# Splitting the first K block's load into four row-quarters and putting one of them ahead of wq in a GQA decode kernel

## The chip, the cores and the metric

The kernel runs on one core of one Trainium2 chip. The metric is the device time of one execution in microseconds. The core has five engines that run side by side and wait for one another through semaphores: PE (matrix products; PEld is its weight load), DVE (vector operations), ACT (activation functions; it also issues DMAs here), POOL and SP (which here only issues DMAs). All DMAs of the core run on the same 16 DMA engines. Data is kept on the chip in 128 partitions.

## The reference

One token `x` of 448 numbers is decoded. An attention part `a` runs over a long cache, a small token mixer `b` runs beside it, and a gate mixes the two.

```python
g = _sigmoid((x * gate_w).sum(-1, keepdims=True))
q = (x @ wq).reshape(B, Sq, Hq, Dh)                # 16 heads of 256
k, v = repeat(k_cache, 2), repeat(v_cache, 2)      # 8 K/V heads, 65536 keys each
scores = einsum("bhqd,bhkd->bhqk", q, k) * (Dh ** -0.5)
a = einsum("bhqk,bhkd->bhqd", _softmax(scores), v).reshape(B, Sq, Hq * Dh) @ wo
h = _layernorm(x)
u = _gelu(einsum("bsd,sf->bdf", h, w1) + b1)       # 1792 wide
b = (einsum("bdf,fs->bds", u, w2) + b2).transpose(0, 2, 1)
out = g * a + (1 - g) * b
```

Nearly all of the bytes are the two caches in bf16: 8 heads x 65536 keys x 256 numbers x 2 bytes, for K and again for V, 537 MB together.

## The kernel before, in words

The keys of each of the 8 K/V heads are cut into 4 blocks of 16384, which makes 32 blocks. A block of K is one transfer of 8 MB: 128 partitions, and in each a row of 64 KB that is contiguous in memory (128 keys of 256 numbers). A block of V is the same.

On the chip there are one buffer `vt` for a block of V and one tile `k_all` with three slots of half a block each (32 KB per partition). A block of K takes two neighbouring slots: even blocks slots 0 and 1, odd blocks slots 1 and 2. DVE transposes a K block in eight pieces (L410, tile `kT`), PE multiplies each piece with the query held in `qz` (L418), and when the eight are done the block's softmax follows (L475 to L514) and the products with V (L438). A loop over t (L605) runs two blocks per pass and 15 passes; the last two blocks are written out behind it.

SP issues all large transfers, in the order in which the program has them: within a block the next V is issued once PE has finished with `vt`, and the next K once DVE has transposed out of the slots that it will overwrite. Transfers that have been issued queue up on the DMA engines, so data flows without a gap as long as the next one is issued before the last has run dry.

Ahead of the loop stands a prelude, and it is what the change touches.

- `xr` (the token) is loaded by ACT's queue, and behind it small tables for the mixer and the gate.
- SP loads `wq` into the space of `vt` that V will use later: a piece `wq_t` of 0.5 MB and a piece `wq_m` of 3 MB (L167, L170). Then it loads K block 0 into slots 0 and 1 of `k_all` (`load_k_whole(0, 0)`, L182, recorded at L132).
- Slot 2 of `k_all` is not needed before block 1. The prelude uses it as scratch under the name `early`: `xf` is the token spread over the partitions (written at L266), `h_bc` its layer norm (L283), `gel` the 14 results of the gelu (ACT, L288), `zt` the gate's product (L346).
- DVE runs the layer norm from L266 to L283 in order; ACT's gelu follows; PE multiplies the queries out of wq (L299, L306), spreads them (L317) and sums the mixer (L352). `gate_sum` ends on ACT with `ez` (L348), and `mixer_tail` on DVE (L357 to L368) finishes the mixer's part.
- A barrier over the engines stands at the loop's entry. In the loop's first half pass PE spreads and applies `wo` (L563, L540, L554), SP issues V block 0 (`load_v`, recorded at L135), and DVE begins to transpose K block 0.

A helper `seq` keeps the instructions of each engine in the order in which they are written, on each side of the loop separately. Which instruction waits for which, and which semaphore it uses, the framework works out from the tiles that each one writes and reads. DMAs take eight semaphores in turn; a DMA that reuses a semaphore first waits for the DMA that had it before.

Of the kernel before, what the change touches and what calls it, by code (L numbers as in the profile page):

```python
# [21 lines left out]
KP = VP // 2  # L22
# [11 lines left out]
def kernel(  # L34
# [15 lines left out]
    nc = tc.nc  # L50
# [12 lines left out]
    def seq(ins):  # L63
        e = ins.ins.engine
        if e in last:
            tc.add_manual_dep(
                ins.ins,
                last[e],
                mybir.DependencyInfo(
                    mybir.DependencyClass.NoSync, mybir.DependencyReason.DATA  # L70
                ),
                reason="program order",
            )
        last[e] = ins.ins.name
        return ins
# [9 lines left out]
    k_all = kvpool.tile([128, 3 * KP, DH], BF16, name="k_all")  # L85
# [24 lines left out]
    DM = 384  # L110
    wq_m = vt[:, 0:48, :].rearrange("p a b -> p (a b)").rearrange("p (k n) -> p k n", k=3)
# [11 lines left out]
    def rows(name, n):  # L123
        return flat[name][bass.ds(n, 1)].rearrange("o p j d -> (o p) j d")
# [6 lines left out]
    def load_k_whole(n, slot):  # L131
        seq(nc.sync.dma_start(out=k_all[:, slot * KP:(slot + 2) * KP, :], in_=rows("k", n)))  # L132

    def load_v(n, j0=0, j1=VP):
        seq(nc.sync.dma_start(out=vt[:, j0:j1, :], in_=rows("v", n)[:, j0:j1, :]))  # L135

# [22 lines left out]
    def load_v_last(n):  # L159
# [4 lines left out]
            ))  # L164

    seq(nc.scalar.dma_start(out=xr[:], in_=A_x[0, 0].rearrange("(o n) -> o n", o=1)))
    seq(nc.sync.dma_start(  # L167
        out=wq_t[:, :], in_=A_wq[DM:D, :].rearrange("r (h n) -> (r h) n", h=2)
    ))
    seq(nc.sync.dma_start(out=wq_m, in_=A_wq[0:DM, :].rearrange("(p k) n -> p k n", k=3)))  # L170
    for k, table in enumerate((
        B_w1[0].rearrange("(b p) -> b p", p=128),
        B_b1.rearrange("(b p) -> b p", p=128),
# [3 lines left out]
    for n0, n1 in ((0, D // 2), (D // 2, D)):  # L177
        seq(nc.scalar.dma_start(
            out=gw[:, n0:n1], in_=gate_w.rearrange("(o n) -> o n", o=1)[:, n0:n1]
        ))  # L180
    seq(nc.scalar.dma_start(out=b2b[:], in_=B_b2.rearrange("(o n) -> o n", o=1)))
    load_k_whole(0, 0)  # L182


    steps = const.tile([128, WS + 128], BF16)
# [8 lines left out]
        out=val[:], in_=rowsel[:, :, :, 0:NI], op=ALU.add, axis=AXIS.XY  # L194
    ))
    fst = const.tile([128, 2, REP], FP32)
    for e in range(2):
        seq(nc.vector.tensor_reduce(
            out=fst[:, e, :], in_=rowsel[:, :, :, e:e + 1], op=ALU.add, axis=AXIS.XY
# [3 lines left out]
        out=par[:], in_=ident_f[:].rearrange("p (a r) -> p r a", r=REP), op=ALU.add, axis=AXIS.X  # L203
# [3 lines left out]
        out=nval[:], in0=val[:], scalar1=-scale, scalar2=None, op0=ALU.mult  # L207
# [7 lines left out]
        out=same[:], in_=val[:].unsqueeze(1).to_broadcast([128, 64, REP])  # L215
# [8 lines left out]
        out=sel[:],  # L224
        in_=ident.rearrange("p (w k) -> p w k", w=NW).unsqueeze(2).to_broadcast([128, NW, NQ, 32]),
# [7 lines left out]
        out=xrr[:], in_=xr[:, DM:D].unsqueeze(2).to_broadcast([1, D - DM, 2])  # L233
    ))
    x_col = hd_ps[:, 40:44]
    for k in range(3):
# [13 lines left out]
        out=xtm[:], in0=par[:], scalar1=x_col[:, 3:4], scalar2=None, op0=ALU.mult  # L250
# [19 lines left out]
        out=veps[:], in0=mv[:, 1:2], scalar1=1e-5, scalar2=None, op0=ALU.add  # L270
# [5 lines left out]
    for _ in range(2):  # L276
# [3 lines left out]
            out=ntmp[:], in0=ntmp[:], scalar1=-0.5, scalar2=1.5, op0=ALU.mult, op1=ALU.add  # L280
# [3 lines left out]
        out=h_bc, in0=xf, scalar1=mv[:, 0:1], scalar2=rstd[:, 0:1],  # L284
        op0=ALU.subtract, op1=ALU.mult,
    ))
    for b in range(NF):
        seq(nc.scalar.activation(  # L288
            out=gel[b], in_=h_bc, func=ACT.Gelu_apprx_tanh,
# [33 lines left out]
    for k in range(2):  # L323
        seq(nc.vector.tensor_copy(
            out=qq[:, :, :, k, :], in_=qq_ps.rearrange("p (w g r) -> p w g r", g=HKV, r=REP)
# [279 lines left out]
    with tc.For_i(0, HQ - 1, 1, iteration_sync="staggered") as t:  # L605
        for e in range(2):
            if e:
                tc.stage_boundary()
            if e == 0:
                spread_wo(1)  # L610
                head_end()
                older_wo()
            tc.previous_stage_wait(mybir.EngineType.Activation)
            score_block(
                e, (e, e + 1), early_signals(0), FORWARD if e else UPPER_FIRST
            )
            load_v(2 * t + e)
            tc.stage_boundary()
            if e == 0:
                load_k_whole(2 * t + 1, 1)  # L620
                load_wo_wide(t)
                softmax(e, may_begin=True)
                tc.previous_stage_wait(mybir.EngineType.DVE)
                tc.previous_stage_wait(mybir.EngineType.Activation)
                products(e)
            else:
                load_k_whole(2 * t + 2, 0)
                softmax(e, pair=t + 1)
                tc.previous_stage_wait(mybir.EngineType.DVE)
                tc.previous_stage_wait(mybir.EngineType.Activation)  # L630
                denominators()
                turn()
                products(e)
# [6 lines left out]
    for n in (L - 1, L):  # L640
# [4 lines left out]
        if n == L - 1:  # L645
            load_v(n, 0, 48)
            load_k(L, 0, 2)
            load_k(L, 1, 1)
            load_v(n, 48, VP)
        else:  # L650
            load_v_last(L)
            load_wo(HQ - 1, 1)
        if n < L:
            softmax(n % 2)
        else:
            def rest_base():
# [9 lines left out]
                out=lsv[:], in0=val[:], scalar1=lsum[:, 0:1], scalar2=None, op0=ALU.mult  # L666
# [8 lines left out]
                out=rdv[:], in0=rdv[:], scalar1=gcol[:, 0:1], scalar2=None, op0=ALU.mult  # L675
# [6 lines left out]
    for c in range(2):  # L682
# [9 lines left out]
        out=oT[:], in0=o_last, in1=rdv[:].unsqueeze(1).to_broadcast([128, 2, REP]), op=ALU.mult  # L692
# [43 lines left out]
```

## Time and profile before

| what | value |
|---|---|
| median of 3 runs | 1263.91 us (1263.62 to 1263.98) |
| span of the profiled execution, first to last instruction | 1261.8 us |
| time around the span (median less span) | 2.1 us |
| DMA | 544.36 MB, mean 431 GB/s over the span |
| PE busy | 824.5 us, 65% of the span |
| DVE busy | 711.8 us, 56% |
| ACT busy | 75.7 us, 6% |
| mean granted PE clock | 0.811 of full |

The profiled execution is one run of the same program; the page gives its span, and its own whole time is not listed beside it, so the span with the 2.1 us around it stands for it. A timeline row reads: start in us, length in us, engine, line, operation, tile written, tile read, how many were merged, and in brackets the idle time in front with what ended it. A row of DMA issues ends with the us from issue to landing.

### The profile page before, as it was taken

How to read it: one execution, taken by the hardware profiler on the slowest of the kernel's cores; microseconds unless marked ns; L12 is line 12 of the kernel's file. 1: busy time of each engine (PE TensorE's matmuls, PEld its weight loads, DVE VectorE, ACT ScalarE, POOL GpSimd, SP SyncE). 2: the span in 40 equal slices, each digit the busy share in tenths (PEclk: the TensorE clock that was granted, in tenths of full speed). 3: DMA queues.
4: the chain of work that ended last, by engine and by line, in shares of the span. 5: the costliest groups of instructions: out<-in, count | busy, mean ns of one | idle time of the engine just before them, and what ended most of it. 6: DMA issues, size and time to landing. Idle time of an engine off the chain costs nothing.

```text
span 1261.8 us, 12358 instructions
## 1 busy us (share of the span) xinstructions
PE 824.5 (65%) x4818; PEld 331.2 (26%) x4818; DVE 711.8 (56%) x755; ACT 75.7 (6%) x163; POOL 4.8 (0%) x9
## 2 busy tenths in 40 slices
PE   4757467575666756577566766658656576665668
PEld 2222122222222312223222322223222232222224
DVE  5665456654556644566544665445655456654575
ACT  4000000000000000000000000000000000000000
POOL 1000000000000000000000000000000000000000
PEclk8887788877787877978778887788877797877878
DMA  9999999999999999999999999999999999999998
GB/s 415 435 435 432 439 432 432 437 434 437 432 434 435 434 425 440 416 441 443 423 434 437 432 432 439 432 439 432 432 439 432 439 432 432 439 432 435 421 435 355
DMA packets 11624, 544.36 MB, mean 431 GB/s; under 512 B 1532, under 2 KB 1918, under 8 KB 2782
## 3 DMA queue, kind: packets, MB, share of 16 engines
q1 hardware_dynamic: 11522, 544.22, 99.6%
q8 instruction: 6, 0.10, 0.0%
q14 instruction: 4, 0.03, 0.0%
q10 hardware_dynamic: 92, 0.01, 0.0%
HBM read 544.22 MB, written 0.00 MB: 431 GB/s over the span
## 4 chain that ended last, share of the span: by engine, by line
DMA 67%; PE 14%; DVE 13%; issue 4%; ACT 0%; SPq 0%; DVEq 0%; ACTq 0%
DMA k_all<-in_A_k_cache_dram 67%; PE sc L418 13%; DVE kT L410 13%; PE hd_ps L463 0%; PE pv_last L438 0%; PE pv_last L563 0%; PE f L563 0%; DVE rmax L475 0%; PE hd_ps L684 0%; ACT p_sb L506 0%; PE hd_ps L554 0%; PE pv_ps L438 0%; PE f L697 0%; PE sm_ps L493 0%; DVE pT L513 0%
## 5 line engine op out<-in xcount | busy, mean ns | idle before, releaser
L418 PE MATMUL sc<-kT,qz 128*128 128x512 bf16 x2048 | 550.4, 419 | 315.0 <-DVE kT L410 314.8
L410 DVE STREAM_TRANSPOSE kT<-k_all 128x2048 f32<-128x2048 f32 x256 | 571.3, 2283 | 207.6 <-DMA k_all<-in_A_k_cache_dram 154.7
L418 PEld LDWEIGHTS <-qz 128*128 128x128 bf16 x2048 | 212.5, 104 | 651.3 <-issue 474.8
L438 PE MATMUL pv_ps<-vt,pT 128*4 128x512 bf16 x1968 | 172.0, 525 | 27.3 <-DVE pT L513 27.3
L519 DVE SCALAR_TENSOR_TENSOR acc<-acc,al,pv_ps 128x512 f32<-128x512 f32 x31 | 23.2, 747 | 160.4 <-PE pv_ps L438 160.4
L438 PEld LDWEIGHTS <-pT 128*4 128x4 bf16 x2000 | 56.5, 108 | 130.1 <-issue 83.9
L506 ACT ACTIVATE p_sb<-sc,nb 128x512 bf16<-128x512 f32 x32 | 22.0, 687 | 1020.0 <-DVE nb L502 1020.0
L475 DVE TENSOR_REDUCE rmax<-sc 128x1 f32<-128x512 f32 x32 | 22.1, 692 | 63.7 <-PE sc L418 63.7
L513 DVE STREAM_TRANSPOSE pT<-p_sb 128x512 bf16<-128x512 bf16 x32 | 22.8, 712 | 27.1 <-ACT p_sb L506 27.1
L525 PE MATMUL hd_ps<-lsum,same 128*128 128x1 f32 x30 | 8.2, 342 | 28.8 <-DVE lsum L514 28.8
L493 PE MATMUL sm_ps<-mrun,ones_f 1*128 1x2 f32 x64 | 12.1, 256 | 21.2 <-DVE mrun L492 13.0
L479 PE MATMUL sm_ps<-ident_f,rmax 128*1 128x128 f32 x32 | 8.6, 270 | 24.5 <-DVE rmax L475 24.5
L563 PE MATMUL pv_last<-wo_in,steps 128*128 128x448 bf16 x64 | 15.6, 368 | 5.5 <-PEq L605 5.5
L563 PEld LDWEIGHTS <-steps 128*128 128x128 bf16 x128 | 11.6, 101 | 22.6 <-issue 14.4
L493 PEld LDWEIGHTS sm_ps<-mrun,ones_f 1*128 1x128 f32 x64 | 9.4, 182 | 27.4 <-DVE mrun L492 16.3
L567 ACT CAST wo_sb<-pv_last 128x448 bf16<-128x448 f32 x16 | 8.5, 532 | 126.3 <-PE pv_last L563 126.3
L558 DVE TENSOR_TENSOR a_acc<-a_acc,hd_ps 1x448 f32<-1x448 f32 x15 | 9.1, 608 | 12.3 <-PE hd_ps L554 12.3
L554 PE MATMUL hd_ps<-wo_sb,oT 128*1 128x448 bf16 x60 | 15.8, 351 | 0.0
L563 PE MATMUL f<-wo_in,steps 128*128 128x448 bf16 x64 | 15.5, 367 | 0.0
L570 ACT COPY wo_sb<-wo_sb 128x896 bf16<-128x896 bf16 x15 | 14.1, 937 | 14.5 <-PE hd_ps L554 14.5
L525 PEld LDWEIGHTS hd_ps<-lsum,same 128*128 128x128 f32 x30 | 6.9, 285 | 30.1 <-DVE lsum L514 30.1
L550 DVE CAST oT<-hd_ps 128x2 bf16<-128x2 f32 x15 | 2.4, 160 | 20.8 <-PE hd_ps L540 20.8
(124 smaller groups left out, 194.6 us busy)
## 6 DMA issues: line engine op xcount, KB each, us to landing
k_all<-in_A_k_cache_dram SPq DMA_DIRECT2D x2, 4096.0 KB, 15.2
vt<-in_A_v_cache_dram SPq DMA_DIRECT2D x1, 5120.0 KB
k_all<-in_A_v_cache_dram SPq DMA_DIRECT2D x1, 4096.0 KB
wo_in<-in_A_wo_dram SPq DMA_DIRECT2D x15, 224.0 KB, 27.8
vt<-in_A_wq_dram SPq DMA_DIRECT2D x1, 3072.0 KB, 10.4
vt<-in_A_v_cache_dram SPq DMA_DIRECT2D x1, 3072.0 KB
k_all<-in_A_v_cache_dram SPq DMA_DIRECT2D x1, 2048.0 KB
k_all<-in_A_v_cache_dram SPq DMA_DIRECT2D x1, 1024.0 KB, 21.7
```

The costliest lines, as they stand in the source:

```text
L410: seq(nc.vector.transpose(out=kT_tiles[i % 2][:].rearrange("p j w k c -> p (j w k c)").bitcast(FP32), in_=slots[pair[i // 4]][:, i % 4 * N ...
L418: seq(nc.tensor.matmul(sc_tiles[e][:, :], lhsT=qz[:, 2 * w + c, 2 * (NI - i):2 * (NI - i) + 128], rhs=kT_tiles[i % 2][:, :, w, :, c], star ...
L438: seq(nc.tensor.matmul(dst[32 * grp:32 * grp + 2 * REP, :, :], lhsT=pT[:, 32 * jj + 2 * REP * ip:32 * jj + 2 * REP * (ip + 1)], rhs=pairs( ...
L475: seq(nc.vector.tensor_reduce(out=rmax[:], in_=sc_ps[:, :], op=ALU.max, axis=AXIS.X))
L493: seq(nc.tensor.matmul(sm_ps[:, 128:128 + REP], lhsT=ones_f[0:1, :], rhs=mrun[0:1, :], start=True, stop=True))
L506: seq(nc.scalar.activation(out=p_sb[:, :], in_=sc_ps[:, :], func=ACT.Exp, scale=scale, bias=nb[:, 0:1], accum_out=den[:, 0:1],))
L513: seq(nc.vector.transpose(out=pT[:, :], in_=p_sb[:, :]))
L519: seq(nc.vector.scalar_tensor_tensor(out=acc[:], in0=acc[:], scalar=al_tiles[e][:, 0:1], in1=src[:, :, :], op0=ALU.mult, op1=ALU.add,))
L525: seq(nc.tensor.matmul(hd_ps[:, 460:461], lhsT=same[:].rearrange("p a r -> p (a r)"), rhs=lsum[:, 0:1], start=True, stop=True,))
L554: seq(nc.tensor.matmul(a_ps, lhsT=oT[:, c, r:r + 1], rhs=wo_sb[:, r, c, :], start=(r == 0 and c == 0), stop=(r == REP - 1 and c == 1),))
L563: seq(nc.tensor.matmul(wo_ps[c], lhsT=steps[:, WS - u:WS - u + 128], rhs=wo_in[:, 2 * u + c, :], start=(u == 0), stop=(u == WS - 1),))
L570: seq(nc.scalar.copy(out=wo_sb[:, 0], in_=wo_sb[:, 1]))
```

## The change

K block 0 is loaded by four transfers instead of one. Each takes every fourth partition (32 rows of 64 KB): rows 0, 4, 8, ... first, then 1, 5, 9, ... and so on. The first of them is issued ahead of both wq pieces, the two wq pieces swap their order, and the other three stand where the whole block's load stood. Nothing else is edited. Lines behind the edit move: what is L266 before is L273 after, L288 is L295, L410 is L417, L605 is L612.

```diff
+    def load_k_rows(b):
+        seq(nc.sync.dma_start(
+            out=k_all[b:128:4, 0:2 * KP, :], in_=rows("k", 0)[b:128:4, :, :]
+        ))
...
     seq(nc.scalar.dma_start(out=xr[:], in_=A_x[0, 0].rearrange("(o n) -> o n", o=1)))
+    load_k_rows(0)
+    seq(nc.sync.dma_start(out=wq_m, in_=A_wq[0:DM, :].rearrange("(p k) n -> p k n", k=3)))
     seq(nc.sync.dma_start(
         out=wq_t[:, :], in_=A_wq[DM:D, :].rearrange("r (h n) -> (r h) n", h=2)
     ))
-    seq(nc.sync.dma_start(out=wq_m, in_=A_wq[0:DM, :].rearrange("(p k) n -> p k n", k=3)))
...
     seq(nc.scalar.dma_start(out=b2b[:], in_=B_b2.rearrange("(o n) -> o n", o=1)))
-    load_k_whole(0, 0)
+    for b in range(1, 4):
+        load_k_rows(b)
```

## The prediction

> **What bounds the kernel now.** I read the page's slices first, then the chain that ended last, then SP's timeline, because the change moves only transfers.
>
> ```profile
> span 1261.8 us, 12358 instructions
> DMA  9999999999999999999999999999999999999998
> GB/s 415 435 435 432 439 432 432 437 434 437 432 434 435 434 425 440 416 441 443 423 434 437 432 432 439 432 439 432 432 439 432 439 432 432 439 432 435 421 435 355
> DMA 67%; PE 14%; DVE 13%; issue 4%; ACT 0%; SPq 0%; DVEq 0%; ACTq 0%
> ```
>
> The DMA engines are busy in every slice, at about 435 GB/s from the second on. The kernel is a stream of 544 MB; it gets shorter only if the stream starts sooner or ends with a shorter tail, and any hole in it is paid in full. So the question is whether the change moves the first byte, or makes a hole. SP's timeline, the issues' landings and the first windows tell how the stream begins:
>
> ```profile
> 0.74 0.42 SPq L167 DMA_DIRECT2D vt<-in_A_wq_dram  x1
> 1.22 0.41 SPq L170 DMA_DIRECT2D vt<-in_A_wq_dram  x1
> 3.98 0.33 SPq L132 DMA_DIRECT2D k_all<-in_A_k_cache_dram  x1
> 27.07 0.35 SPq L135 DMA_DIRECT2D vt<-in_A_v_cache_dram  x1
> 43.98 0.34 SPq L132 DMA_DIRECT2D k_all<-in_A_k_cache_dram  x1
> 63.47 0.35 SPq L135 DMA_DIRECT2D vt<-in_A_v_cache_dram  x1
> ...
> vt<-in_A_wq_dram SPq DMA_DIRECT2D x1, 3072.0 KB, 10.4
> vt<-in_A_wq_dram SPq DMA_DIRECT2D x1, 512.0 KB, 3.2
> k_all<-in_A_k_cache_dram SPq DMA_DIRECT2D x1, 28.1
> vt<-in_A_v_cache_dram SPq DMA_DIRECT2D x1, 24.3
> ...
> 1.00:2.00 1.00, 0.00 (x0) 0.00 (x0) 0.00 (x0) 0.00 (x0) 0.98 (x1) 1.00 0.16 54
> ```
>
> K block 0 is issued at 3.98 and lands 28.1 later, at 32.1. V block 0 is issued at 27.07, 5.0 us before that, and lands at 51.4, 19.3 after K: 8.39 MB at 435 GB/s, so no hole lies between them. In the second microsecond the stream moves 54 GB/s, 0.12 us worth, so data begins at 1.88, 1.14 after the issue at 0.74.
>
> What lets SP issue V block 0 at 27.07 is the end of the prelude:
>
> ```profile
> 8.53 0.62 DVE L266 COPY k_all<-sm_ps 128x448 f32<-128x448 f32 x1
> 10.37 0.16 DVE L274 CAST w2b<-hd_ps 128x14 bf16<-128x14 f32 x1
> 11.69 0.16 PEld L299 LDWEIGHTS <-vt 128*128 128x128 bf16 x3 [1.58 <-DMA vt<-in_A_wq_dram]
> 12.79 9.23 ACT L288 ACTIVATE k_all<-k_all,wb 128x448 bf16<-128x448 f32 x14 [1.02 <-DVE k_all L283]
> 15.30 0.19 DVE L314 CAST qb<-hd_ps 128x32 bf16<-128x32 f32 x1 [2.55 <-PE hd_ps L306]
> 15.75 4.74 PE L352 MATMUL f<-k_all,w2b 128*1 128x448 bf16 x11
> 22.03 1.28 ACT L348 ACT_TABLE_LOAD   x1
> 23.33 0.20 ACT L348 ACTIVATE ez<-z 1x1 f32<-1x1 f32 x1
> 23.56 0.14 DVE L357 TENSOR_SCALAR gate<-ez 1x1 f32<-1x1 f32 x1 [3.19 <-ACT ez L348]
> 25.30 0.61 DVE L368 TENSOR_TENSOR rest<-y_sb,rest 1x448 f32<-1x448 f32 x1
> ```
>
> The layer norm starts at 8.53, the gelu runs from 12.79 to 22.02, the gate ends at 23.53 on ACT and the mixer's tail at 25.91 on DVE. The barrier and V's issue follow 1.16 later.
>
> **The change, part by part.** The built program of the changed kernel, engine by engine with its waits, shows more than the diff:
>
> ```
> SP   k_all<-in_A_k_cache 32x32768
> SP   vt<-in_A_wq 128x12288        [waits DMAHW0]
> SP   vt<-in_A_wq 128x2048         [waits DMAHW1]
> SP   k_all<-in_A_k_cache 32x32768 [waits DMAHW2]
> SP   k_all<-in_A_k_cache 32x32768 [waits DMAHW3]
> SP   k_all<-in_A_k_cache 32x32768 [waits DMAHW4]
> DVE  L273 k_all<-sm_ps 128x448 [waits DMAHW3,DMAHW2,DMAHW4,DMAHW1,PE]   (before: L266 [waits PE])
> ACT  L295 LoadActFuncSet       [waits DMAHW3,DMAHW2,DMAHW4,DMAHW1]      (before: L288, no wait)
> ```
>
> DMAHW1 to 4 are the semaphores of the four quarters, and the values waited for (32 on three that a small table used before, 16 on the first) are reached only when each quarter has landed. DVE's write of `xf` goes to slot 2, the quarters to slots 0 and 1. I take it that the framework treats a destination of every fourth partition as the whole stretch of addresses from its first row to its last, which crosses slot 2. The bytes don't collide; the wait is there all the same. It is the largest step of the change.
>
> *1. The new wait.* L266, at 8.53 before, can't start until all of K block 0 is in, 32.1 plus 0.1 for two semaphore waits. Behind it on DVE stand the whole layer norm, the query copies and the gate; behind those ACT's gelu, PE's queries (their first product waits for the cast at L274) and the barrier. From L266 to the end of `ez` takes 23.53 - 8.53 = 15.0, and nothing in it was waiting for a DMA but the query products (11.69, 3.16 after L266), which have wq long before now: they may start at 2.0 after L266, when L274 is done. The chain through the gelu stays the longest.
>
> *2. The mixer's tail moves.* In the built program L357 to L368 stand behind the loop. That takes 2.35 us (23.56 to 25.91) off the prelude and puts it here:
>
> ```profile
> 1192.23 0.75 DVE L519 SCALAR_TENSOR_TENSOR acc<-acc,al,pv_ps 128x512 f32<-128x512 f32 x1 [5.36 <-PE pv_ps L438]
> 1195.02 0.66 DVE L588 SCALAR_TENSOR_TENSOR y_sb<-a_acc,gate,rest 1x448 f32<-1x448 f32 x1
> 1199.77 4.50 DVE L410 STREAM_TRANSPOSE kT<-k_all 128x2048 f32<-128x2048 f32 x2 [4.08 <-DMA k_all<-in_A_k_cache_dram]
> ```
>
> DVE waits 4.08 us for K there; 2.35 us more fit. Cost nothing; without that cover 2.35.
>
> *3. V block 0's issue.* 32.2 + 15.0 + 1.16 = 48.4 instead of 27.07. The stream, which ran through 32.1 before, now ends there and starts again 1.14 after the issue, at 49.5. The last byte of a transfer comes before its landing: wq's 0.5 MB landed 3.2 after its issue, of which 1.14 is the start and 1.2 the bytes at 435 GB/s, so 0.86 is the end. The hole runs from 32.1 - 0.86 = 31.2 to 49.5: 18.3 us.
>
> *4. Later issues.* The engines' work moves with V's issue, by 21.3; data moves by 18.3. K block 1 is issued 16.9 after V block 0, at 65.3, while V's data runs to 49.5 + 19.3 = 68.8: in time. V block 1 comes at 63.47 + 21.3 = 84.8, and K block 1's data ends at 88.1: in time by 3.3, of which 1.14 is the start. After that both are as before. The hole is not made up: the slices show no slack in the stream.
>
> *5. Order and size of the early transfers.* The first issue stays at 0.74, so the first byte gains nothing. The sum of bytes is the same. wq_m waits for DMAHW0, the semaphore of `xr`, which PE had at 2.03:
>
> ```profile
> 2.03 0.10 PEld L237 LDWEIGHTS <-xr 1*128 1x128 bf16 x1 [2.03 <-DMA xr<-in_A_x_dram]
> ```
>
> If it lands then, wq_m is queued 4 us ahead of the quarter's end (1.88 + 2.1 MB at 435 GB/s = 6.7). If it waits behind both 64 KB rows that its DMA engine holds (435 / 16 = 27 GB/s for an engine, so 4.8 us for two) it lands near 6.8 and wq_m starts at 8.0, a hole of 1.3. I take 0, since the row is a direct one, and keep 0 to 1.3. wq_t waits for the quarter, some 7.5, while wq_m runs to about 14; quarters 1 to 3 follow as SP gets there. Six issues of 0.3 to 0.4 us each are covered by data in flight.
>
> Whether 32 rows on every fourth partition run at full rate is not seen at this size. The nearest rows are those of `wo`, 32 rows on every fourth partition, 229 KB, in the odd passes of the chain:
>
> ```profile
> 43.98 26.68 DMA k_all<-in_A_k_cache_dram
> 81.59 28.19 DMA k_all<-in_A_k_cache_dram
> 120.50 27.89 DMA k_all<-in_A_k_cache_dram
> 159.69 27.87 DMA k_all<-in_A_k_cache_dram
> ```
>
> K landed at 70.66, 109.78, 148.39 and 187.56: 39.12, 38.61, 39.17 apart. The longer gaps hold a `wo`, and the 0.51 to 0.56 is 229 KB at 410 to 450 GB/s. So full rate, 0; at half rate four quarters would need 19.3 more, which is the other end.
>
> *6. PE's clock.* PE will have stood idle for over 20 us when the queries start. After a shorter gap the trace shows
>
> ```profile
> 12.00:16.00 4.00, 3.72 (x128) 3.45 (x126) 1.02 (x5) 3.21 (x5) 0.00 (x0) 1.00 1.06 459
> 24.00:26.00 2.00, 0.00 (x0) 0.00 (x0) 1.73 (x3) 0.00 (x0) 0.00 (x0) 0.50 1.21 524
> ```
>
> a granted clock of 1.00 while the queries ran and 0.50 in the gap. At half clock the queries' 3.6 us (11.69 to 15.30, where DVE takes them over) could become 7.2. They start 2.0 after L266 and would end at 9.2; 0.45 later (15.30 to 15.75) the mixer's 14 sums begin, 0.43 each by the 11 that took 4.74, and end at 15.7 after L266, 0.7 behind `ez`. I take 0, since the clock may rise on the way, and keep 0 to 1.
>
> [...]
>
> *Sum.* 18.3 + 0 + 0 + 0. The profiled span goes from 1261.8 to 1280.1; the median lies 2.1 above the span (1263.91), so 1282.2, taken as 1282, 1.4% slower.
>
> **The rivals.** *Slow quarters, 7%.* [...] Against: `wo` above. 5 to 19 us on top: 1287 to 1301.
>
> [...]
>
> *Small holes on top, 7%.* `xr` late (1.3), PE cold (1), V block 1 late (its 2.2 us of reserve gone): together up to 4, 1283 to 1286.
>
> *The wait is there but partly hidden, 2%.* If the gelu's chain is shorter than its rows say, or V's issue doesn't need the whole of it, the hole shrinks in proportion; halved, 1273.
>
> *Not slower, 2%.* If V block 0 were issued by the time K's last byte is in, there would be no hole. It decides at an issue at or before 31.2 - 1.14 = 30.1; the chain of 15.0 + 1.16 would have to start at 13.9, with K not yet half in. Only waits satisfied by other means allow that. The price is then what the first transfer's larger rows bring to the start, at most the 0.74 to 1.88 that precede the first byte: 1262.8 to 1263.9.
>
> **How the numbers follow.** The forecast has 82%: 1282, its own range 1279 (a chain 2 shorter and a block landed 1 sooner) to 1285. With the small holes 1286; the range 1277 to 1290 takes in part of the slow quarters and of the half-hidden wait, and leaves out about 1 in 10. A measurement here can tell 0.2%, 2.5 us. Slower by more: 0.82 + 0.07 + 0.07 + 0.02 - 0.01 = 0.97; within 0.2%: 0.02; faster: 0.01.
>
> **What would show it.** In the changed kernel's profile L273 on DVE should start just after 32 with its idle time ended by the DMA into `k_all`; the gelu should run near 36.5 to 45.7; V block 0 should be issued near 48.4; the second slice (31.5 to 63) should drop from 435 GB/s to about 180 to 200, with all others as before, and the first stay near 415. The mixer's tail should appear after 1210. The prediction is wrong if V's issue stays near 27, or if K lands well after 34.

## The result and the profile after

The changed kernel takes 1282.96 us (median of 4 runs, 1282.62 to 1283.18) against 1263.91 before: 19.05 us more, a ratio of 1.015 with a 95% interval of 1.0137 to 1.0162. It is slower, by about what the prediction gave (1282).

The page of the changed kernel, span and slices:

```profile
span 1281.4 us, 12364 instructions
DMA  8599999999999999999999999999999999999998
GB/s 377 228 431 430 426 433 438 437 438 430 433 426 433 454 433 430 426 433 444 439 430 430 433 426 441 446 430 433 426 433 454 433 428 428 433 440 435 420 439 346
```

The second slice, 32 to 64 us, was at 435 GB/s before and is at 228 now; from the third on the stream is as full as it was. Nearly all of the loss lies at the start. The stretches there, by a windows view of the changed kernel (stretch, busy time of PE, PEld, DVE, ACT, POOL, granted PE clock, DMA share, GB/s):

```profile
8.00:30.00 22.00, 0.69 (x3) 0.25 (x4) 0.30 (x2) 0.00 (x0) 0.00 (x0) 1.00 1.02 441
30.00:47.00 17.00, 10.84 (x147) 4.97 (x147) 8.00 (x35) 12.20 (x18) 0.00 (x0) 1.00 0.00 1
```

For 22 us the DMA engines are full and the other engines do next to nothing; for the next 17 the engines work and hardly any data moves. (The view counts a row of K where it begins. Each trace also holds the DMA packets one by one, a row of 64 KB being one packet, and by these the last rows of K begin at 28.2 to 29.0 us and end at 30.7 to 31.4.) Before, the two ran side by side: in the same two stretches the stream moved 436 GB/s, and PE was busy for 12.82 and 13.13 us. The timeline of the changed kernel says why (SP's, DVE's, PE's and ACT's rows):

```profile
0.74 0.57 SPq L135 DMA_DIRECT2D k_all<-in_A_k_cache_dram  x1
2.00 0.39 SPq L173 DMA_DIRECT2D vt<-in_A_wq_dram  x1
8.83 0.33 SPq L174 DMA_DIRECT2D vt<-in_A_wq_dram  x1
9.21 2.70 SPq L135 DMA_DIRECT2D k_all<-in_A_k_cache_dram  x3
46.89 0.36 SPq L140 DMA_DIRECT2D vt<-in_A_v_cache_dram  x1
64.72 0.34 SPq L132 DMA_DIRECT2D k_all<-in_A_k_cache_dram  x1
84.11 0.35 SPq L140 DMA_DIRECT2D vt<-in_A_v_cache_dram  x1
...
31.79 0.62 DVE L273 COPY k_all<-sm_ps 128x448 f32<-128x448 f32 x1 [23.35 <-DMA k_all<-in_A_k_cache_dram]
33.71 0.22 PE L306 MATMUL hd_ps<-xm,vt 128*128 128x1 bf16 x3 [21.85 <-DVE w2b L281]
37.30 0.19 DVE L321 CAST qb<-hd_ps 128x32 bf16<-128x32 f32 x1 [1.30 <-PE hd_ps L313]
...
36.04 9.23 ACT L295 ACTIVATE k_all<-k_all,wb 128x448 bf16<-128x448 f32 x14 [1.02 <-DVE k_all L290]
46.58 0.20 ACT L355 ACTIVATE ez<-z 1x1 f32<-1x1 f32 x1
```

DVE's write of the scratch (L273) waits 23.35 us for the DMA into `k_all` and starts at 31.79 instead of 8.53. The gate ends at 46.78, V block 0 is issued at 46.89 instead of 27.07.

From the chain that ended last, the pieces of waiting for K in the changed kernel (start, length):

```profile
64.72 24.64 DMA k_all<-in_A_k_cache_dram
99.89 28.59 DMA k_all<-in_A_k_cache_dram
139.67 27.50 DMA k_all<-in_A_k_cache_dram
177.70 28.66 DMA k_all<-in_A_k_cache_dram
```

K blocks 1 to 4 land at 89.36, 128.48, 167.17 and 206.36. Before they landed at 70.66, 109.78, 148.39 and 187.56. Each is 18.7 or 18.8 later, and so is a block of K near the end (1218.43 against 1199.67): the hole is made once, and the loop neither adds to it nor heals it. The two spans differ by 19.6 us, more than the medians, in part because the profiled execution of the changed kernel was its slowest run (1283.18). In that kernel's runs the time lies 1.7 to 1.8 us above the span, so the 2.1 given for the kernel before most likely sets a median beside the span of a faster run; the forecast, a difference, doesn't depend on it.

### The profile page after: what moved, and what is told of

Same layout as the page of the kernel before. It is cut to its first block, busy times and chain, and to the rows that moved or that the text cites. A ratio compares the mean times of both kernels' runs of the same rounds, so it can differ in the third digit from the quotient of the medians.

```text
span 1281.4 us, 12364 instructions
## 1 busy us (share of the span) xinstructions
PE 821.4 (64%) x4818; PEld 330.4 (26%) x4818; DVE 711.0 (55%) x755; ACT 75.7 (6%) x163; POOL 4.8 (0%) x9
## 4 chain that ended last, share of the span: by engine, by line
DMA 68%; DVE 12%; PE 12%; issue 4%; SPq 0%; ACT 0%; DVEq 0%
DMA k_all<-in_A_k_cache_dram 66%; DVE kT L417 12%; PE sc L425 11%; DMA k_all<-in_A_v_cache_dram 2%; PE pv_last L570 0%; PE hd_ps L561 0%; PE f L570 0%; SPq L166 0%; PE f L704 0%; SPq L132 0%; PE sm_ps L547 0%; ACT p_sb L513 0%; DVE rmax L482 0%; PE hd_ps L547 0%; PE sm_ps L500 0%
## 5 line engine op out<-in xcount | busy, mean ns | idle before, releaser
L425 PE MATMUL sc<-kT,qz 128*128 128x512 bf16 x2048 | 544.2, 415 | 318.1 <-DVE kT L417 317.9
L417 DVE STREAM_TRANSPOSE kT<-k_all 128x2048 f32<-128x2048 f32 x256 | 570.7, 2283 | 204.8 <-DMA k_all<-in_A_k_cache_dram 156.1
L306 PE MATMUL hd_ps<-xm,vt 128*128 128x1 bf16 x96 | 3.5, 165 | 21.8 <-DVE w2b L281 21.8
```

The lines of the kernel that those rows point to most:

```text
L417: seq(nc.vector.transpose(out=kT_tiles[i % 2][:].rearrange("p j w k c -> p (j w k c)").bitcast(FP32), in_=slots[pair[i // 4]][:, i % 4 * N ...
L425: seq(nc.tensor.matmul(sc_tiles[e][:, :], lhsT=qz[:, 2 * w + c, 2 * (NI - i):2 * (NI - i) + 128], rhs=kT_tiles[i % 2][:, :, w, :, c], star ...
```

## The experiments

Three questions were open: is it the wait or the order of the transfers; is a stepped quarter slow by itself; and from which moment on does a late V block 0 cost time?

**The wait taken away.** The scratch goes into the part of `vt` that wq leaves free; its bytes are then far from every quarter, and the framework makes no wait. Order and sizes stay as in the changed kernel.

```diff
-    early = slots[2].rearrange("p j d -> p (j d)")
+    early = vt[:, 56:VP, :].rearrange("p j d -> p (j d)")
```

> The changed kernel with its prelude's scratch moved from slot 2 of k_all into the part of vt that wq leaves free; order and size of the transfers stay. Theory (the wait on the quarters makes the hole): the layer norm starts near 8.5 again instead of 31.8, V block 0 is issued between 25 and 27 while K is still in flight, and the time is that of the kernel before, 1263.5 to 1264.5 us. Rival (order or size of the early transfers cost the time): V's issue moves but the time stays near 1283. Rival (the quarters are slow or leave small holes that the large one covered): 1265 to 1283, with K block 0 landing later than 32.1.

Measured: 1266.38 us, ratio to before 1.002 (1.0011 to 1.0029). 16.6 of the 19.05 us are gone with one line. 2.3 are left against the kernel before that ran alongside (1264.05), which the theory did not expect. Its timeline (SP, PE, DVE, ACT):

```profile
31.20 0.36 SPq L140 DMA_DIRECT2D vt<-in_A_v_cache_dram  x1
...
11.48 0.19 PE L270 MATMUL hd_ps<-steps,tables 42*128 42x42 bf16 x1 [2.99 <-DMA tables<-in_B_w_dram]
16.17 0.24 PE L306 MATMUL hd_ps<-xm,vt 128*128 128x1 bf16 x3 [4.50 <-DMA vt<-in_A_wq_dram]
17.38 0.19 PE L313 MATMUL hd_ps<-xtm,vt 128*128 128x1 bf16 x1 [0.97 <-DMA vt<-in_A_wq_dram]
20.91 0.19 DVE L321 CAST qb<-hd_ps 128x32 bf16<-128x32 f32 x1 [6.78 <-PE hd_ps L313]
25.37 0.61 DVE L354 TENSOR_REDUCE z<-vt 1x1 f32<-1x448 f32 x1
27.59 0.14 DVE L364 TENSOR_SCALAR gate<-ez 1x1 f32<-1x1 f32 x1 [1.61 <-ACT ez L355]
27.35 0.20 ACT L355 ACTIVATE ez<-z 1x1 f32<-1x1 f32 x1
```

V's issue is at 31.20, not between 25 and 27. wq comes behind a quarter of K, so the queries start at 16.17 instead of 11.69 and wait once more for `wq_t` (until 17.38), and what follows them on DVE ends at 25.98; now the gate waits for that and no longer for the gelu (done at 23.40). The small tables also land later (PE waits for them until 11.48, against 10.03 before). The new order has a price of its own, part of which the large wait had covered. One thing differs besides the wait: the mixer's tail, which the changed kernel has behind the loop, stands ahead of it here, as in the kernel before (L364 at 27.59). So 3.65 us pass from the gate's end to V's issue, 0.11 in the changed kernel.

**The control.** The same line in the kernel before.

> The kernel before with the same move of the scratch, as a control for the run with the changed kernel. Theory: nothing waits differently, V block 0 is issued near 27.1, 1263.9 us, within 0.1%. Rival (the move itself matters, since V block 0 now waits for DVE and ACT as well): V is issued later than 30.1 and the time goes above 1265.

Measured: 1264.01 us, ratio 1.0 (0.9991 to 1.0009), V issued at 27.66. Moving the scratch shifts V's issue by 0.6 us and changes nothing in the time.

**The order without stepped partitions.** The first transfer takes a quarter of the keys of every partition; wq follows, then the rest of K.

```diff
-            out=k_all[b:128:4, 0:2 * KP, :], in_=rows("k", 0)[b:128:4, :, :]
+            out=k_all[:, j0:j1, :], in_=rows("k", 0)[:, j0:j1, :]
...
+    load_k_cols(0, KP // 2)
...
+    load_k_cols(KP // 2, 2 * KP)
```

> The same order as in the changed kernel, but the first transfer is a quarter of the keys of every partition (128 rows of 16 KB) and the other three quarters come as one transfer behind wq. No destination steps over partitions and the scratch stays in slot 2. Theory (the stepped destination brings the wait): no wait on K at the layer norm, V issued near 27, 1263.5 to 1264.5 us. Rival (putting K ahead of wq makes the hole): near 1283.

Measured: 1265.72 us, ratio 1.0014 (1.0005 to 1.0023). Its timeline:

```profile
30.26 0.35 SPq L140 DMA_DIRECT2D vt<-in_A_v_cache_dram  x1
...
8.53 0.62 DVE L272 COPY k_all<-sm_ps 128x448 f32<-128x448 f32 x1
```

The layer norm starts at 8.53, as the theory had it, so the wait belongs to the stepped destination, and not to K standing first. The time and V's issue miss the theory: again the order alone costs some 1.7 us, since the queries start at 15.30 and V is issued at 30.26.

**The stepped quarters alone, twice.** wq first as before, K in four stepped quarters behind it; once with the scratch in slot 2, once in `vt`.

```diff
...
-    load_k_whole(0, 0)
+    for b in range(4):
+        load_k_rows(b)
```

> The kernel before, with wq first as it was, and K block 0 in four quarters of every fourth partition behind it: the stepped destinations alone. Theory (the wait is all): the layer norm starts when K has landed, near 32, V is issued near 47 and the time is that of the changed kernel, 1282 to 1284. Rival (the order does it): 1264.

Measured: 1281.86 us, ratio 1.0143 (1.0126 to 1.016). Its timeline:

```profile
4.22 6.14 SPq L135 DMA_DIRECT2D k_all<-in_A_k_cache_dram  x4
46.24 0.36 SPq L140 DMA_DIRECT2D vt<-in_A_v_cache_dram  x1
...
31.12 0.62 DVE L272 COPY k_all<-sm_ps 128x448 f32<-128x448 f32 x1 [22.69 <-DMA k_all<-in_A_k_cache_dram]
```

The stepped destination is enough; the order is not needed for the loss. The same kernel with the scratch in `vt`:

> The kernel before, wq first, with K block 0 in four quarters of every fourth partition behind it and the scratch moved to vt: the stepped quarters without the wait and without the new order. Theory (the stepped quarters cost nothing by themselves, the 2.3 us left in the first run come from wq standing behind the first quarter): V issued near 27.7 as in the control, the queries' first product near 11.7, 1264.0 us. Rival (the quarters leave holes of their own): 1265.5 to 1266.5 with V issued before 28.5.

Measured: 1264.33 us, ratio 1.0002 (0.9993 to 1.0011). Its timeline:

```profile
27.20 0.36 SPq L140 DMA_DIRECT2D vt<-in_A_v_cache_dram  x1
```

Four stepped quarters behind wq, without the wait, are as fast as one transfer (1264.33 against 1263.99 for the kernel before alongside). With the kernels above this closes the square: wait and order both absent 1264, order alone 1266, wait alone 1282, both 1283. The two don't add up, because the order's delay of the queries is spent while the wait lasts: in the changed kernel they start at 33.71, released by DVE (L281), with wq long there. In both kernels with the wait the mixer's tail stands behind the loop, in both without it ahead of the loop.

**Neighbouring partitions instead of every fourth.**

```diff
-            out=k_all[b:128:4, 0:2 * KP, :], in_=rows("k", 0)[b:128:4, :, :]
+            out=k_all[32 * b:32 * b + 32, 0:2 * KP, :], in_=rows("k", 0)[32 * b:32 * b + 32, :, :]
```

> The changed kernel with the quarters taken as 32 neighbouring partitions each instead of every fourth. Theory (the stepped destination brings the wait): the layer norm starts near 8.5 and V is issued near 27, so the hole of 18 us goes. If 32 neighbouring partitions take data as fast as every fourth, 1264. If they take it at half rate, each 2.1 MB quarter needs 9.6 instead of 4.8 us where nothing else fills in, and the time is 1264 plus up to 19. Rival (four transfers instead of one make the wait, however they are cut): L273 starts only when K has landed, 1283 or more.

Measured: 1285.37 us, ratio 1.0169 (1.0153 to 1.0185). Its timeline, and then its DMA view of the stretch from 20 to 53 us:

```profile
0.73 0.40 SPq L135 DMA_DIRECT2D k_all<-in_A_k_cache_dram  x1
13.30 0.34 SPq L174 DMA_DIRECT2D vt<-in_A_wq_dram  x1
...
8.53 0.62 DVE L273 COPY k_all<-sm_ps 128x448 f32<-128x448 f32 x1
53.71 4.50 DVE L417 STREAM_TRANSPOSE kT<-k_all 128x2048 f32<-128x2048 f32 x2 [11.15 <-DMA k_all<-in_A_k_cache_dram]
```

```profile
DMA packets 265, 7.72 MB, mean 234 GB/s; under 512 B 64, under 2 KB 64, under 8 KB 151
```

The wait is gone (L273 at 8.53), so four transfers as such don't make it, and the time is worse all the same: 21.3 us above the kernel before, 2 more than the half rate of the expectation allowed. The stream runs at 234 GB/s instead of 435 while the quarters are in flight, though the DMA engines count as busy: by the packets a row of 64 KB takes 5.1 us on its engine instead of 2.4. wq_t, which waits for the first quarter, is issued at 13.30 against 8.83 with every fourth partition: 4.5 later, and at half rate 2.1 MB take 4.8 us more. K lands shortly before 53.71, where DVE's wait for it ends. So the rival of slow quarters is real for this cut and didn't arise for the other.

What in 32 neighbouring partitions makes a row take 5.1 us, and in every fourth 2.4, was not tried.

**Where a late V begins to cost.** The kernel before with some gelu activations done again, the same result in the same place, so that only ACT's chain grows.

```diff
-    for b in range(NF):
+    for b in list(range(4)) + list(range(NF)):
         seq(nc.scalar.activation(
             out=gel[b], ...
```

> The kernel before, with four gelu activations done once more (same input, same place): ACT's chain is 4 x 0.66 = 2.6 us longer. V block 0 is issued near 29.7 instead of 27.1. Theory (only an issue later than 30.1 makes a hole): 1263.9, no change. Rival (any delay of V's issue is paid): 1266.5.

Measured: 1265.52 us, ratio 1.0014 (1.0005 to 1.0024). A miss: V is issued at 29.65, ahead of the 30.1 that the prediction gave, and yet it costs 1.6. Its timeline, and then its DMA issues with the us to landing:

```profile
4.31 0.33 SPq L132 DMA_DIRECT2D k_all<-in_A_k_cache_dram  x1
29.65 0.35 SPq L135 DMA_DIRECT2D vt<-in_A_v_cache_dram  x1
```

```profile
k_all<-in_A_k_cache_dram SPq DMA_DIRECT2D x1, 28.0
```

K lands at 32.3, 2.7 after V's issue, and there is a loss nonetheless. The packets show why. Fifteen of the 16 DMA engines end their last row of K at 30.2 to 30.6 us and one at 32.0, and the landing follows the last of them; the mean is 30.5. And a V that finds the engines idle, as in the two runs that follow, begins 1.2 to 1.3 us after its issue on average, with first rows of 3.1 us instead of 2.4. So its issue has to come by about 30.5 - 1.25 - 0.65 = 28.6. A rougher sum leads to nearly the same place: 12.06 MB of wq and K at 435 GB/s from 1.88 on end at 29.6, and less 1.14 for V's start that is 28.5. By the packets its end is 0.9 too early and its start 0.8 too short, so part of its agreement is luck; the runs below decide between 28.5 and 30.1. With all 14 done twice and three times (`list(range(NF)) * 3`):

> The kernel before with all 14 gelu activations done twice: 9.2 us more on ACT. The mixer's tail stands behind the loop here, as in the changed kernel, so V block 0 is issued some 0.1 after the gate ends, near 32.9. Theory (the hole is what V's issue is later than 30.1): 2.8 us, 1266.7. Rival (all delay from 27.1 on is paid): 1269.7. Rival (delays of the prelude are made up later in the loop): 1263.9.

> The kernel before with all 14 gelu activations done three times: 18.5 us more on ACT, V block 0 issued near 42.1. Theory: a hole of 42.1 - 30.1 = 12.0 us, 1275.9. Rival (all delay from 27.1 on is paid): 1278.9. Rival (made up later): 1263.9.

Measured: 1268.09 (ratio 1.0033, 1.002 to 1.0046) with V at 32.74, and 1277.33 (1.0105, 1.0088 to 1.0122) with V at 41.90. V's issue in the first and in the second:

```profile
32.74 0.35 SPq L135 DMA_DIRECT2D vt<-in_A_v_cache_dram  x1
...
41.90 0.35 SPq L135 DMA_DIRECT2D vt<-in_A_v_cache_dram  x1
```

Between the two, 9.16 us of delay cost 9.24: one for one. Both are 1.4 above what a bound of 30.1 gives and fit 28.5. This was tried on its own:

> The kernel before with two gelu activations done once more, 1.3 us on ACT: V block 0 issued near 28.4. Theory (over the runs so far the time follows V's issue one for one from 28.5 on, where the stream's bytes at 435 GB/s run out less the 1.1 us that a transfer takes to start): 1263.9 to 1264.1, no change. Rival (the bound lies lower and any delay from 27.1 on is paid): 1265.2.

Measured: 1264.13 us, ratio 1.0004 (0.9995 to 1.0013). Its timeline:

```profile
28.40 0.35 SPq L135 DMA_DIRECT2D vt<-in_A_v_cache_dram  x1
```

By the median, 1.3 us of delay are free, as 28.5 says. But the runs spread: six of the 11 took 1263.71 to 1264.13 and five 1264.76 to 1266.83, while the slowest of the kernel before alongside took 1264.90. The execution with this profile took 1265.24; in it five of the 16 DMA engines begin V only at 31.8 to 32.5 us, and only one of them still had K to move until then. So 28.4 lies on the edge and is not free in every run. An issue at 27.7, in the control above, is.

All kernels in one table; the last column is 1277.33 plus the distance of V's issue from 41.90, and 1264.0 up to an issue at 28.5:

| kernel | V block 0 issued (us) | measured (us) | one for one from 28.5 |
|---|---|---|---|
| before | 27.07 | 1263.91 | 1264.0 |
| stepped quarters behind wq, scratch in vt | 27.20 | 1264.33 | 1264.0 |
| before, scratch in vt | 27.66 | 1264.01 | 1264.0 |
| before, 2 more gelu | 28.40 | 1264.13 | 1264.0 |
| before, 4 more gelu | 29.65 | 1265.52 | 1265.1 |
| quarter of the keys first | 30.26 | 1265.72 | 1265.7 |
| changed, scratch in vt | 31.20 | 1266.38 | 1266.6 |
| before, gelu twice | 32.74 | 1268.09 | 1268.2 |
| before, gelu three times | 41.90 | 1277.33 | 1277.3 |
| stepped quarters behind wq | 46.24 | 1281.86 | 1281.7 |
| changed | 46.89 | 1282.96 | 1282.3 |

One number, read off SP's timeline, carries ten of the eleven kernels to within 0.45 us; two of the ten, the first row and 1277.33, fix the line. The changed kernel stands 0.6 above its line, about the spread of its own runs (1282.62 to 1283.18). By the packets its V block 0 ends 18.4 us later than before (68.2 against 49.8), just as its issue says, so the 0.6 arise behind V block 0; where is not known. The kernel with neighbouring partitions is not on the line, since there the stream itself is slow. No kernel tried is faster than before.

## Why the prediction was right

**The new wait (1)** was right in place and size. L273 waited for K and started at 31.79 (32.2 forecast), and from there to the end of the gate it took 14.99 (15.0). Its cause is shown as far as experiments go: with a stepped destination and the scratch in the same tile the wait is there, without either of the two it isn't. That the framework takes the stepped rows as one stretch of addresses is an inference. The forecast's 0.1 for two semaphore waits was an estimate that no run shows on its own; in the kernel before, rows of such waits take 21 ns (L410, the median) and 51 ns (L352). The signs named for the new wait came: the gelu at 36.04 to 45.27 (36.5 to 45.7), the tail behind 1210. The first two slices are at 377 and 228 GB/s (415, and 180 to 200 forecast): the stream ends at 31 and not at 32, and V is issued sooner.

**The mixer's tail (2)** stands behind the loop and is hidden, as forecast. The changed kernel's DVE there:

```profile
1210.51 0.14 DVE L364 TENSOR_SCALAR gate<-ez 1x1 f32<-1x1 f32 x1
1212.84 0.67 DVE L595 SCALAR_TENSOR_TENSOR y_sb<-a_acc,gate,rest 1x448 f32<-1x448 f32 x1
1218.45 4.50 DVE L417 STREAM_TRANSPOSE kT<-k_all 128x2048 f32<-128x2048 f32 x2 [4.94 <-DMA k_all<-in_A_k_cache_dram]
```

DVE is done at 1213.5 and waits 4.94 us for K.

**V's issue and the hole (3)** came out at 18.3 by errors that cancel, and that is luck. The issue is at 46.89, not 48.4: L273 was 0.4 sooner, and the barrier cost 0.11 behind the gate instead of 1.16, which belonged to the mixer's tail in front of it. That makes the hole 1.5 us shorter. Terms that the sum left out make it as much longer. By the packets the engines are idle for 17.1 us on average, from 31.0, where K's last rows end (31.2 forecast), to 48.1, where V's first begin. Those first rows take 3.2 us instead of 2.5, which adds 0.7. And K's last rows end 0.55 later than in the kernel before (30.4). 17.1 + 0.7 + 0.55 = 18.4, and the bound found above says the same: 46.89 - 28.5 = 18.4. The 30.1 that the prediction gave for the last free issue has the same fault: it left out the slower first rows, and took one end of K, 31.2, where that of the kernels with wq first is 30.5.

**Later issues (4)** were in time: K block 1 at 64.72 (65.3), V block 1 at 84.11 (84.8), and the shift of the landings stays at 18.7 to 18.8.

**Order and size (5)** were taken at 0, with 0 to 1.3 for a late `xr`. `xr` landed in time (wq_m issued at 2.00): its packet moves at 1.65, ahead of K's first rows at 2.10, and whether its being a direct row matters, the reason given for the 0, no run shows. The stepped quarters run at full rate behind wq (1264.33 without the wait). But the order isn't quite free even here: with the wait alone (1281.86) the kernel is 1.1 us faster than with both, and K's rows end 0.6 sooner (30.4). What the step missed besides is that wq behind 2.1 MB of K delays the queries by 4.5 us. That is worth 2.3 us as soon as the wait is gone.

**PE's clock (6)** cost nothing: the queries took 3.59 us (33.71 to 37.30) against 3.61 before. The fear rested on a granted clock of 1.00 for them before; the matmul groups say otherwise (behind the count, the shortest, median and longest in ns). Before, and then after:

```profile
L352 PE MATMUL f<-k_all,w2b x14: 349/554/577, 15.7 to 22.1; 128*1 128x448 bf16 x14
```

```profile
L359 PE MATMUL f<-k_all,w2b x14: 529/532/577, 37.7 to 45.4; 128*1 128x448 bf16 x14
L570 PE MATMUL pv_last<-wo_in,steps x64: 349/353/581, 46.9 to 1211.1; 128*128 128x448 bf16 x64
```

A product of 448 columns has a median of 554 ns in the prelude of before and 532 in that of after, against 353 in the loop. So PE was slow in most of both preludes, whatever the windows' clock says there. Nor did it get faster on the way, as the prediction thought it might: the last product of the changed kernel's prelude began at 45.4, and none took less than 529.

**The rivals.** Slow quarters and small holes on top did not come; the half-hidden wait and the kernel that is not slower fell with L273 at 31.79. The point at which the last of them decides was given as an issue at 30.1; it is 28.5.

## What to carry to other kernels

Before splitting a transfer, look at the built program's waits for whatever else lives in the destination's tile: a wait on bytes that never collide costs time all the same (here 16.6 of the 19.05 us), and it appeared on scratch in a tile that DMAs fill. In a kernel bound by its stream, find the issue that keeps the stream fed, and ask when it has to come: by the mean end of the bytes in flight, less the start of a transfer, and not by the landing of the last one (here 28.5 us, with the landing at 32.1). In this case the quarters of 32 neighbouring partitions ran at 234 GB/s, about half rate, and those of every fourth partition at 441 (8 to 30 us); but the step brought the wait, and a cut by columns brought neither.

## What the runs showed that was not expected

The landing of a transfer overstated here how long the stream is fed. K block 0 lands at 32.1 to 32.3 in the kernels with wq first, but its last rows end at 30.5 on the mean of the 16 DMA engines, and a V block issued 2.7 us ahead of that landing still costs 1.6.

Small transfers beside 64 KB rows landed late here, though less for the rows' sake than it seems. The mixer's three tables, issued by 2.8 us, reach PE at 11.67 in the changed kernel, at 11.48 with its scratch moved, at 16.99 with neighbouring partitions, and at 9.13 where the first rows are 16 KB. But they reach it at 10.03 in the kernel before too, where no row of 64 KB begins ahead of 10.7. Before, and then after:

```profile
10.03 0.19 PE L263 MATMUL hd_ps<-steps,tables 42*128 42x42 bf16 x1 [1.54 <-DVE mv L268]
```

```profile
11.67 0.19 PE L270 MATMUL hd_ps<-steps,tables 42*128 42x42 bf16 x1 [3.17 <-DMA tables<-in_B_w_dram]
```

(The first row names DVE's `mv`, which the product doesn't read; the tables' last packet ends at 9.5, 0.5 ahead of it.) By the packets the three tables move one after another, 1.8 to 2.6 us apart, in both kernels: they begin at 4.3, 6.2 and 8.0 before and at 5.0, 7.6 and 9.4 after. What makes that spacing was not tried. The rest, 11.67 against 10.03 at PE, comes with the rows of K. In the changed kernel each of the 14 engines that carry the tables moves a row of K (until 5.0 to 5.9 us), then its part of the first table, then a second row of K (until 7.6 to 8.3), then its part of the second table. With neighbouring partitions both rows of K go ahead of the first table, which begins at 11.8; why two there is open.
